# Attention units of one PSUM bank in a fused attention and gated MLP kernel

## The chip, the cores and the metric

The kernel runs on one core of a Trainium2 chip. The metric is the time of the device in microseconds (us). Five engines work beside each other and meet only at semaphores: TensorE (PE: matmuls; PEld: its weight loads), VectorE (DVE), ScalarE (ACT), GpSimd (POOL), and SyncE (SP), which issues the DMAs. A PSUM bank is here a tile of 128 partitions by 512 float32 values; eight of them are allotted.

## The reference

Attention over 4 batches of 8 heads, 1152 keys and values of 64 numbers each; queries are averaged in pairs, which leaves 576. Its output feeds a gated MLP with a residual (cut to what matters):

```python
q_pool = q.reshape(B, H, S // 2, 2, D).mean(axis=3)           # 4, 8, 576, 64
scores = scale * q_pool @ k.transpose(0, 1, 3, 2)             # 576 x 1152 per head
attn = softmax(scores)                                         # over the 1152 keys
x = (attn @ v) -> (B, 576, 512)
u, v = split(gelu(x @ w_in))                                   # 512 each
v_s = einsum("ts,bsd->btd", w_sg, layernorm(v) * g_ln) + b_sg
out = x + (u * v_s) @ w_out
```

## The kernel before

**Units.** The 32 heads stand in 16 pairs p of two heads. A head's 1152 keys are KJ = 9 tiles of 128. One step of attention, `attend(g)`, is a head with one key tile j, so g runs over 288 units. A unit holds all 576 queries, in a score tile of two PSUM banks with 288 columns in each (pool "S", two tiles of two banks). TensorE writes the scores in two passes, `scores(0)` and `scores(1)` (line 450), the second of which adds low-order parts and subtracts each query's maximum; ScalarE takes the exponential (line 458). In pairs 0 and 2 (`F32P`, "wide") the exponential stays float32 and TensorE weighs v with it (line 496, five blocks of 128 queries). In the other pairs it is split into two float16 parts: ScalarE makes the first (line 472, into a tile f of pool "F"), and the second, the residual, is made on VectorE for every other unit, which is "kept": its exponential is written back into the score tile, which stays taken until the residual is done. For the rest the exponential goes to a tile e of pool "E" in SBUF, the score tile is free after it, and GpSimd makes the residual (both line 477). TensorE then weighs v with both parts (line 489, 15 matmuls per unit) into one bank, `avp`, which sums a head's nine units and is emptied by ScalarE (line 523), divided on VectorE and GpSimd.

The 576 queries are four blocks of 128 and a last of 64. In the unit before, the 64 lead the row, so that the fifth block is a 128-column slice that starts with them.

**What goes before a unit.** For each pair: loads of k, q, v (`load`), scales (`scales`), splitting k, q and v in two parts (`prepare`, lines 319 to 340 on ScalarE, VectorE and SP; `values`, 362 and 365), transposition by DMA, a copy of k's second half, and the maxima (`maxima`): TensorE writes 128 x 512 raw scores into a bank (line 389), VectorE reduces it (line 395, tile mp), GpSimd splits the maximum, and a DMA transposes it into q2, without which `scores(1)` can't start.

**Other work.** The gated MLP of a batch (`project`, `gmlp`, matmuls in `unit`, line 634) is mixed into the attention of the next one; only that of the last batch stands alone at the end. At the start `spatial` loads and splits the gate weights w_sg (line 880 and on; residuals on VectorE in line 947) and `weights` splits w_in and w_out.

**Order.** Nothing runs in the order of the source. `Schedule.add` notes each piece with an engine, an estimated duration, what it reads and writes, a due time and a pool from which it takes a buffer; `Schedule.run` then plays all engines forward and always starts the ready piece with the earliest due time. The engine queues are fixed by that before the kernel runs. The due times come from the tables D_... at the end of the file (`lead`), one number per kind of work and pair. The pieces "sseq", "eseq", "fseq" and "avp" keep scores, exponentials, first parts and weighing each in the order of the units. The banks of PSUM: `avp` 1, S 2 x 2, X 2 (maxima, transpositions, MLP), M 1.

## Time and profile before

| | |
|---|---|
| median of 3 runs | 675.05 us (673.8 to 675.7) |
| span of the profiled execution | 671.1 us |
| median less that span | 3.95 us |
| busy: TensorE, VectorE, ScalarE, GpSimd | 630.2, 531.6, 520.0, 365.4 us |
| mean granted clock of TensorE | 0.997 |

For the profiled execution the page gives the span, from its first to its last instruction, and no time of its own beside it; the difference to the median stands in the third line. Busy times are sums over the span: an engine that is 79% busy over the whole can be full for 50 us. A TensorE that counts as busy is not at its peak, since ends of matmuls are modelled; the spacing of starts tells more. Idle time of an engine matters only where the engine that ends the stretch waits for it.

### The profile page before, as it was taken

The numbers are of one execution on the slowest core, as the hardware profiler recorded it, in microseconds if no ns is written. First come the engines' busy times: TensorE is split into PE (matmuls) and PEld (weight loads), VectorE is DVE, ScalarE is ACT, GpSimd is POOL, SyncE is SP. The second block draws the span as 40 slices with busy tenths as digits, with TensorE's granted clock in tenths as the row PEclk, the third lists the DMA queues.
The fourth block names the chain that finished last, engine by engine and source line by source line (L and its number), as shares of the span: only waits on it lengthen the run. The fifth ranks groups of instructions, "written<-read, shape, count | busy, mean of one in ns | idle before, by whom it ended". The sixth has DMA issues, their size and how long they took to land.

```text
span 671.1 us, 18518 instructions
## 1 busy us (share of the span) xinstructions
PE 630.2 (94%) x7498; PEld 492.5 (73%) x7498; DVE 531.6 (79%) x1066; ACT 520.0 (77%) x851; POOL 365.4 (54%) x425
## 2 busy tenths in 40 slices
PE   3889879988999999999999999999999999999997
PEld 1578658966777876867777986687777976887955
DVE  4979999798988997888988898888888897243462
ACT  6477988699989789889999888978987797773220
POOL 6243865547464558736465556874444467640172
PEclk9899999999999999999999999999999999999999
DMA  8797847544443315655356223529333200010002
GB/s 231 206 246 161 218 70 213 123 80 111 127 97 84 77 22 143 105 143 126 88 130 144 48 72 66 110 71 220 79 68 72 49 11 17 7 49 23 1 1 71
DMA packets 110133, 66.78 MB, mean 100 GB/s; under 512 B 88480, under 2 KB 92576, under 8 KB 109920
## 3 DMA queue, kind: packets, MB, share of 16 engines
q1 hardware_dynamic: 110048, 65.61, 41.3%
q8 instruction: 58, 0.95, 0.6%
q14 instruction: 27, 0.22, 0.1%
HBM read 36.23 MB, written 4.72 MB: 61 GB/s over the span
## 4 chain that ended last, share of the span: by engine, by line
PE 68%; DVE 15%; ACT 7%; DMA 5%; issue 3%; POOL 2%; SPq 0%; ACTq 0%; POOLq 0%; DVEq 0%
PE s L450 15%; PE pm L634 13%; PE avp L489 12%; PE px L634 11%; PE px L389 7%; DVE mp L395 5%; PE avp L496 4%; DVE f L477 2%; DMA k<-kn 2%; ACT f L472 2%; ACT e L458 1%; ACT s L458 1%; DMA kr<-in_k_dram 1%; DVE va L365 1%; DVE t L673 1%
## 5 line engine op out<-in xcount | busy, mean ns | idle before, releaser
L477 POOL TENSOR_TENSOR f<-e,f 128x576 f16<-128x576 f32 x126 | 166.2, 1319 | 139.2 <-ACT f L472 128.7
L450 PE MATMUL s<-q,k 128*128 128x288 f16 (+2 forms) x1440 | 216.4, 262 | 10.4 <-ACT e L458 6.3
L395 DVE TENSOR_REDUCE mp<-px 128x1 f32<-128x512 f32 (+2 forms) x304 | 193.0, 661 | 23.1 <-PE px L389 22.8
L489 PEld LDWEIGHTS <-f 128*128 128x128 f16 x3780 | 147.4, 97 | 24.1 <-issue 3.8
L489 PE MATMUL avp<-va,f 128*128 128x65 f16 x3780 | 157.1, 193 | 2.3 <-POOL f L477 1.8
L450 PEld LDWEIGHTS <-k 128*128 128x128 f16 x1440 | 105.0, 98 | 67.2 <-issue 34.6
L477 DVE TENSOR_TENSOR f<-s,f 128x576 f16<-128x576 f32 x126 | 94.4, 749 | 37.3 <-ACT f L472 37.2
L389 PE MATMUL px<-k,q 128*128 128x512 f16 (+1 forms) x437 | 114.8, 326 | 7.5 <-DVE mp L395 5.2
L458 ACT ACTIVATE e<-s 128x576 f32<-128x576 f32 x162 | 104.8, 648 | 18.7 <-PE s L450 13.2
L458 ACT ACTIVATE s<-s 128x576 f32<-128x576 f32 x126 | 81.1, 644 | 36.5 <-PE s L450 35.3
L472 ACT ACTIVATE f<-e 128x576 f16<-128x576 f32 x126 | 86.7, 688 | 4.1
L472 ACT ACTIVATE f<-s 128x576 f16<-128x576 f32 x126 | 81.9, 650 | 2.6 <-PE avp L489 0.5
L389 PEld LDWEIGHTS <-q 128*128 128x128 f16 x480 | 43.0, 100 | 21.8 <-issue 12.0
L496 PEld LDWEIGHTS avp<-va,e 128*128 128x128 f32 x360 | 43.7, 192 | 2.1 <-ACT a L523 1.2
L496 PE MATMUL avp<-va,e 128*128 128x65 f32 x360 | 44.4, 271 | 0.4 <-ACT a L523 0.4
L314 POOL TENSOR_TENSOR qs<-qr 128x256 f32<-128x256 f32 x32 | 25.6, 801 | 34.9 <-DVE n L336 19.5
L634 PE MATMUL pm<-win_h,xg 128*128 128x512 f32 x104 | 38.7, 417 | 0.0
L634 PEld LDWEIGHTS <-vz 128*128 128x128 f16 x224 | 20.5, 98 | 19.3 <-POOL vz L681 1.1
L530 POOL TENSOR_TENSOR x<-a,dn 128x320 f32<-128x320 f32 x32 | 25.7, 803 | 15.9 <-DVE dn L527 14.0
L634 PE MATMUL px<-wsg,vz 128*128 128x512 f16 x126 | 32.5, 379 | 0.8 <-POOL vz L681 0.6
L634 PE MATMUL pm<-xg,win_h 128*128 128x288 f32 x144 | 31.1, 308 | 0.7 <-DVE u L606 0.7
L322 DVE SCALAR_TENSOR_TENSOR kn<-kr,sc,kn 128x576 f16<-128x576 f32 x32 | 28.8, 909 | 1.4 <-ACT kn L319 1.4
(162 smaller groups left out, 1095.3 us busy)
## 6 DMA issues: line engine op xcount, KB each, us to landing
kr<-in_k_dram SPq DMA_DIRECT2D x16, 576.0 KB, 4.7
qr<-in_q_dram SPq DMA_DIRECT2D x16, 512.0 KB, 4.1
vr<-in_v_dram SPq DMA_DIRECT2D x14, 576.0 KB, 4.0
k<-k SPq DMA_DIRECT2D x32, 144.0 KB, 2.6
x<-in_moe_w_in_dram SPq DMA_DIRECT2D x8, 512.0 KB, 5.9
out_dram<-t SPq DMA_DIRECT2D x16, 256.0 KB, 2.1
x<-in_moe_w_out_dram SPq DMA_DIRECT2D x8, 256.0 KB, 3.2
u<-in_moe_w_sg_dram SPq DMA_DIRECT2D x1, 1152.0 KB, 6.5
```

Of the source, the lines that this page charges most:

```text
L314: nc.gpsimd.tensor_tensor(out=qs[:, 6 * h:6 * h + 4, :], in0=qr[:, h, :, 0, :], in1=qr[:, h, :, 1, :], op=ALU.add)
L322: nc.vector.scalar_tensor_tensor(out=kn[:, h, :, 1, :], in0=kr[:, h], scalar=s[:, 0:1], in1=kn[:, h, :, 0, :], op0=ALU.mult, op1=ALU.subtract)
L389: nc.tensor.matmul(out=bank(x)[:, w * i:w * i + w], lhsT=q1[c][:, o, :], rhs=k1[c][:, h, j0:j0 + nj, :].rearrange("p j k -> p (j k)"), sta ...
L395: nc.vector.tensor_reduce(out=mp[c][:, r0:r0 + len(group), g], in_=src, axis=AX.X, op=ALU.max)
L450: nc.tensor.matmul(out=buf(("s", g))[:, a, to:to + n], lhsT=kk[c][:, hh, j, :], rhs=qq[:, at:at + n], start=(i == 0 and to == 0), stop=(i ...
L458: nc.scalar.activation(out=s if kept else halves(buf(("e", g))), in_=s, func=AF.Exp, scale=SCALE * 2.0**-ASH)
L472: nc.scalar.activation(out=f, in_=exponentials(), func=AF.Copy)
L477: eng.tensor_tensor(out=halves(f[:, 1]), in0=exponentials(), in1=halves(f[:, 0]), op=ALU.subtract)
L489: nc.tensor.matmul(out=avp[:, o:o + m], lhsT=w[:, col:col + 128], rhs=vv, start=(j == 0 and n == 0 and x == 0), stop=(j == KJ - 1 and n == ...
L496: nc.tensor.matmul(out=avp[:, o:o + D + 1], lhsT=e[:, col:col + 128], rhs=vj, start=(j == 0 and n == 0), stop=(j == KJ - 1 and n == 4), sk ...
L530: nc.gpsimd.tensor_tensor(out=xbuf[b % 2][:, :, col], in0=a[:, :, 0:D], in1=d.rearrange("p (i o) -> p i o", o=1).to_broadcast([128, 5, D]) ...
L634: nc.tensor.matmul(out=bank(m)[:, 0:cols], lhsT=l, rhs=r, start=(k + j == 0), stop=(k + j == n - 1))
```

## The change

A unit is now one bank: 512 queries of a key tile. The last 64 queries are gathered over key tiles: after j = 4 a tail unit takes those of tiles 0 to 4 side by side (320 columns), after j = 8 those of tiles 5 to 8 (256 columns). A head thus has 11 units, 9 main and 2 tail. Each tail block brings its own k tile as weights in the score matmuls and its own v tile in the weighing. Every other main unit is kept as before; tail units never are (`KEEPT`), so their residuals are made on GpSimd. A slice of 128 columns at the end of a tail unit reaches 64 columns beyond it, into columns that must hold numbers: GpSimd sets columns 256 to 383 of all E and F tiles to zero once at the start (`clear`), and the first score pass of every unit waits for it.

The seven banks beside `avp` become seven tiles of one bank, 3 S, 3 X and 1 M, in place of two pairs and three. All due times of the tables are new, so the queues of all engines stand in another order.

```diff
-        "S": tiles(psum, 2, [128, 2, 512], F32, "s"),
+        "S": tiles(psum, NPS, [128, 512], F32, "s"),
         "X": tiles(psum, NXB, [128, 512], F32, "px"),
-        "M": tiles(psum, 3 - NXB, [128, 512], F32, "pm"),
+        "M": tiles(psum, 7 - NPS - NXB, [128, 512], F32, "pm"),
...
     def attend(g):
         h, j = divmod(g, KJ)
         p, hh = divmod(h, 2)
...
+        main(g, h, p, hh, j)
+        if j in TAILS:
+            j0 = max([0] + [a + 1 for a in TAILS if a < j])
+            unit_of(("t", g), g + TOFF, h, p, hh, [(i, 4, 64 * (i - j0)) for i in range(j0, j + 1)])
+        if j < KJ - 1:
+            return
+        heads_end(g, h, p, hh)
+
+    def main(g, h, p, hh, j):
+        unit_of(g, g, h, p, hh, [(j, i, 128 * i) for i in range(4)])
+
+    def unit_of(u, g, h, p, hh, blocks):
...
+        tail = blocks[0][1] == 4
+        n = 64 * len(blocks) if tail else TM
+        o = (704 if hh else TM) if tail else 768 * hh
...
-            parts = [(0, 0, o, HALF), (1, 0, o + HALF, HALF)] if hh else [(0, 0, TM, TT), (0, TT, 0, HALF - TT), (1, 0, HALF - TT, HALF)]
-            for a, to, at, n in parts:
-                nc.tensor.matmul(out=buf(("s", g))[:, a, to:to + n], lhsT=kk[c][:, hh, j, :], rhs=qq[:, at:at + n],
-                                 start=(i == 0 and to == 0), stop=(i == 1 and to + n == HALF), skip_group_check=True)
+            for m, (j, _, col) in enumerate(blocks if tail else blocks[:1]):
+                w = TT if tail else TM
+                nc.tensor.matmul(out=buf(("s", u))[:, col:col + w], lhsT=kk[c][:, hh, j, :], rhs=qq[:, o:o + w],
+                                 start=(i == 0 and m == 0), stop=(i == 1 and col + w == n), skip_group_check=True)
...
-        kept = not wide and share(g, KEEP[p >= NP])
+        kept = not wide and (share(int(g), KEEP[p >= NP]) if not tail else KEEPT)
...
+        def clear():
+            for t in pools["F"]:
+                nc.gpsimd.memset(t[:, :, 256:384], 0.0)
+            for t in pools["E"]:
+                nc.gpsimd.memset(t[:, 256:384], 0.0)
...
-D_LK = (-94.74, -97.1, -50.09, -46.73, -13.16)
+D_LK = (-874.76, -83.67, 106.62, 781.44, 481.99)
...
-NXB = 2
+NXB = 3
+NPS = 3
+TAILS, TOFF, KEEPT = (4, 8), 0.5, False
```

Exponential, first part, residual and weighing run over the n columns of a unit and, in the weighing, over its blocks; else they are as before.

Three places show what the new table does to the queues. The first is VectorE's queue where pair 3 ends and pair 4 begins: f is the unit's float16 tile, s its score tile, kn and n2 the second parts of the next pair's k and q, mp the reductions, pm and sc the scales. Before:

```order
L477 TENSOR_TENSOR f3_131<-s0_134,f3_131 128x576
L322 SCALAR_TENSOR_TENSOR kn_94<-kr_90,sc2_106,kn_94 128x9x64
L336 SCALAR_TENSOR_TENSOR n2_85<-qs_83,sc2_106,n1_84 128x5x64 x2
L395 TENSOR_REDUCE mp1_82<-px1_137 128x1
L271 TENSOR_SCALAR pm1_103<-pm0_138 128x1
L272 TENSOR_SCALAR pm1_103<-pm1_103 128x1
L293 RECIPROCAL sc5_109<-pm1_103 128x1
L296 TENSOR_SCALAR sc5_109<-sc5_109 128x1
L395 TENSOR_REDUCE mp1_82<-px0_136 128x1
L395 TENSOR_REDUCE mp1_82<-px1_137 128x1
L477 TENSOR_TENSOR f1_129<-s1_135,f1_129 128x576
```

And now, from the same residual (the 18th that VectorE makes):

```order
L482 TENSOR_TENSOR f2_130<-s2_136,f2_130 128x512
L859 SCALAR_TENSOR_TENSOR x1_89<-x1_89 128x256
L862 SCALAR_TENSOR_TENSOR x1_89<-x1_89 128x256
L482 TENSOR_TENSOR f1_129<-s0_134,f1_129 128x512
L533 TENSOR_SCALAR dn1_115<-a1_113,sc3_107 128x5
L534 RECIPROCAL dn1_115<-dn1_115 128x5
L364 SCALAR_TENSOR_TENSOR va0_86<-vr_91,sc4_108,va0_86 128x9x64
L482 TENSOR_TENSOR f3_131<-s2_136,f3_131 128x512
L335 SCALAR_TENSOR_TENSOR n2_85<-qs_83,sc2_106,n1_84 128x5x64 x2
L321 SCALAR_TENSOR_TENSOR kn_94<-kr_90,sc2_106,kn_94 128x9x64
```

The two residuals, the 18th and the 19th, stood nine rows apart; now two short ones on w_out's parts (x1) stand between them, and the parts of q and k come after the 20th.

The second is SP's queue at the start of the program, where kr, qr, qe and va are k, q, q's last rows and v of pair 0, and the rows from in_moe_w_sg to g_ln are the gate's. Before:

```order
L240 DMA kr_90<-in_k_dram 128x2x576
L243 DMA qr_92<-in_q_dram 128x2x512
L246 DMA qe_93<-in_q_dram 64x128 x2
L880 DMA u_97<-in_moe_w_sg_dram 128x2304
L883 DMA x1_89<-in_moe_w_sg_dram 64x576
L884 DMA x1_89<-in_moe_b_sg_dram 128x576
L885 DMA graw_141<-in_moe_g_ln_dram 128x4x1
L340 DMA_TRANSPOSE q10_77<-n1_84 128x5x128
L326 DMA_TRANSPOSE k10_73<-kn_94 128x9x128 x2
```

And now:

```order
L239 DMA kr_90<-in_k_dram 128x2x576
L895 DMA u_97<-in_moe_w_sg_dram 128x2304
L898 DMA x1_89<-in_moe_w_sg_dram 64x576
L899 DMA x1_89<-in_moe_b_sg_dram 128x576
L900 DMA graw_143<-in_moe_g_ln_dram 128x4x1
L242 DMA qr_92<-in_q_dram 128x2x512
L245 DMA qe_93<-in_q_dram 64x128 x2
L253 DMA va0_86<-in_v_dram 128x9x64 x2
L325 DMA_TRANSPOSE k10_73<-kn_94 128x9x128
```

The loads of q moved behind those of the gate, and the load of v came ahead of the first transposition.

The third is ScalarE's queue in pair 4: e<-s and s<-s are exponentials, f<-s and f<-e first parts; the number behind s is the score tile. Before:

```order
L458 ACTIVATE s1_135<-s1_135 128x2x288
L472 ACTIVATE f3_131<-s1_135 128x576
L458 ACTIVATE e2_126<-s0_134 128x576
L841 ACTIVATE x1_89<-x1_89,ebias_64 128x256
L472 ACTIVATE f0_128<-e2_126 128x576
L458 ACTIVATE s0_134<-s0_134 128x2x288
L472 ACTIVATE f1_129<-s0_134 128x576
L458 ACTIVATE e1_125<-s1_135 128x576
L472 ACTIVATE f2_130<-e1_125 128x576
```

And now:

```order
L471 ACTIVATE e0_124<-s1_135 128x512
L477 ACTIVATE f0_128<-e3_127 128x320
L471 ACTIVATE s0_134<-s0_134 128x512
L856 ACTIVATE x1_89<-x1_89,ebias_64 128x256
L477 ACTIVATE f1_129<-e0_124 128x512
L471 ACTIVATE e1_125<-s1_135 128x512
L477 ACTIVATE f2_130<-s0_134 128x512
L471 ACTIVATE s2_136<-s2_136 128x512
```

Two score tiles took turns; now three do, and a first part of a tail (320 columns) stands among those of 512.

## Rows read from the trace of the kernel before

**Rows 1.** Page, engines: busy us (share of the span) xinstructions.

```profile
PE 630.2 (94%) x7498; PEld 492.5 (73%) x7498; DVE 531.6 (79%) x1066; ACT 520.0 (77%) x851; POOL 365.4 (54%) x425
```

**Rows 2.** Stretches: span; busy us (x) of PE, PEld, DVE, ACT, POOL; granted clock, DMA, GB/s.

```profile
0.00:13.90 13.90, 3.02 (x17) 2.56 (x18) 4.87 (x22) 9.54 (x14) 8.75 (x14) 1.00 0.83 245
13.90:50.00 36.10, 31.95 (x211) 21.91 (x210) 32.23 (x66) 19.92 (x34) 13.45 (x20) 0.95 0.89 220
50.00:97.30 47.30, 41.49 (x530) 33.45 (x531) 45.23 (x88) 40.02 (x67) 28.49 (x36) 1.00 0.66 154
97.30:167.00 69.70, 63.10 (x755) 52.03 (x752) 59.93 (x126) 57.86 (x101) 41.49 (x52) 1.00 0.54 129
167.00:607.30 440.30, 433.02 (x5651) 339.39 (x5650) 361.80 (x715) 378.18 (x619) 254.14 (x289) 1.00 0.37 86
607.30:671.00 63.70, 57.57 (x342) 43.22 (x340) 27.52 (x53) 14.44 (x19) 19.09 (x17) 1.00 0.07 23
```

**Rows 3.** Waits: engine, line waited for: us in total, times, longest us.

```profile
PE s L450 <- ACT e L458: 6.3, 11, 1.2
...
PE px L389 <- DVE mp L395: 5.2, 8, 1.8
...
PE s L450 <- DVE f L477: 3.4, 9, 0.8
```

**Rows 4.** Timeline of TensorE at 401 us: start, us, instruction, tiles, shape, count.

```profile
401.21 0.62 PE L489 MATMUL avp<-va,f 128*128 128x65 f16 x15
401.67 0.41 PE L450 MATMUL s<-q,k 128*128 128x288 f16 x2
401.92 0.38 PE L389 MATMUL px<-k,q 128*128 128x512 f16 x1
402.13 0.44 PE L489 MATMUL avp<-va,f 128*128 128x65 f16 x9
```

**Rows 5.** VectorE's groups by shape: line, tiles, shape, count; busy us, mean ns; idle before.

```profile
L395 DVE TENSOR_REDUCE mp<-px 128x1 f32<-128x512 f32 x259 | 170.6, 681 | 21.1 <-PE px L389 20.9
L477 DVE TENSOR_TENSOR f<-s,f 128x576 f16<-128x576 f32 x126 | 94.4, 749 | 37.3 <-ACT f L472 37.2
L322 DVE SCALAR_TENSOR_TENSOR kn<-kr,sc,kn 128x576 f16<-128x576 f32 x32 | 28.8, 909 | 1.4 <-ACT kn L319 1.4
...
L336 DVE SCALAR_TENSOR_TENSOR n<-qs,sc,n 128x320 f16<-128x320 f32 x32 | 23.6, 748 | 2.6 <-DMA q<-n 1.4 <-ACT n L332 1.1
```

**Rows 6.** Timeline of VectorE, residuals 9, 18 and 19, and TensorE's wait between.

```profile
96.53 0.74 DVE L477 TENSOR_TENSOR f<-s,f 128x576 f16<-128x576 f32 x1
...
160.45 0.76 DVE L477 TENSOR_TENSOR f<-s,f 128x576 f16<-128x576 f32 x1 [1.63 <-ACT f L472]
...
166.24 0.75 DVE L477 TENSOR_TENSOR f<-s,f 128x576 f16<-128x576 f32 x1
...
164.54 0.38 PE L389 MATMUL px<-k,q 128*128 128x512 f16 x1 [1.19 <-DVE mp L395]
```

**Rows 7.** ScalarE's and GpSimd's groups by shape, columns as in rows 5.

```profile
L458 ACT ACTIVATE e<-s 128x576 f32<-128x576 f32 x162 | 104.8, 648 | 18.7 <-PE s L450 13.2 <-PE avp L496 3.6 <-DVE f L477 0.8
...
L523 ACT ACTIVATE a<-avp 128x325 f32<-128x325 f32 x32 | 14.1, 442 | 3.1 <-PE avp L489 3.1
...
L477 POOL TENSOR_TENSOR f<-e,f 128x576 f16<-128x576 f32 x126 | 166.2, 1319 | 139.2 <-ACT f L472 128.7 <-PE s L450 8.3 <-POOL qs L316 1.3
...
L850 POOL TENSOR_TENSOR x<-x 128x256 f32<-128x256 f32 x8 | 6.1, 764 | 6.7 <-DVE x L847 6.7
```

**Rows 8.** Timeline of the start: TensorE, GpSimd, and one row of VectorE.

```profile
13.90 0.58 PE L389 MATMUL s<-k,q 128*128 128x512 f16 x1 [0.86 <-DMA k<-kn]
...
6.28 0.72 POOL L314 TENSOR_TENSOR qs<-qr 128x256 f32<-128x256 f32 x1 [4.41 <-DMA qr<-in_q_dram]
...
8.73 2.01 POOL L782 MEMSET k<- 64x2304 f16 x1
...
21.11 0.74 DVE L947 SCALAR_TENSOR_TENSOR wsg<-px,wsc,wsg 128x512 f16<-128x512 f32 x1
```

More of the change, by code (lines that the diff above doesn't have):

```diff
@@ L463, in exponentials @@
         def exponentials():
[L465 removed]
+            return (buf(("s", u)) if kept else buf(("e", u)))[:, 0:n]
         def exp_hi():
[L468 to L472 removed]
+            nc.scalar.activation(out=buf(("f", u))[:, 0, 0:n], in_=exponentials(), func=AF.Copy)
@@ L492, in weigh_wide @@
         def weigh_wide():
-            e, vj = buf(("e", g)), vw[c][:, KJ * hh + j, :]
-            for n, (i, col) in enumerate(blocks):
+            e = buf(("e", u))
+            for k, (j, i, col) in enumerate(blocks):
                 o = (D + 1) * i
-                nc.tensor.matmul(out=avp[:, o:o + D + 1], lhsT=e[:, col:col + 128], rhs=vj, start=(j == 0 and n == 0),
-                                 stop=(j == KJ - 1 and n == 4), skip_group_check=True)
-        hi_dve = not kept and share(g, E1F[p >= NP])
@@ L500, in attend @@
-        home = ("s", g) if kept else ("e", g)
-        add("PE", 0.246, lambda: scores(0), r=[f"k1{c}{hh}", f"q1{c}{hh}"] + ([f"q1{c}0"] if hh else []), w=["sseq", f"s{g}"], due=g - 0.8,
-            acq=(("s", g), ["S"]))
-        add("PE", 0.246, lambda: scores(1), r=[f"k2{c}{hh}", f"q2{c}{hh}", f"k2z{c}"], w=[f"s{g}"], due=g - 0.7)
+                nc.tensor.matmul(out=avp[:, o:o + D + 1], lhsT=e[:, col:col + 128], rhs=vw[c][:, KJ * hh + j, :],
+                                 start=(j == 0 and k == 0 and not tail), stop=(j == KJ - 1 and tail), skip_group_check=True)
```

106 lines of the change are left out of this document (53 added, 53 removed).

## The prediction

> **What bounds the kernel now.** I read the busy times first, then the span cut into stretches, then the waits, and last two close-ups. TensorE is busy 630.2 of 671.1 us [rows 1], so at most 40.9 us can be won without taking matmuls away, and the change takes hardly any. The question is only where TensorE stands idle and what it waits for there. The stretches [rows 2] give its idle time as length minus busy: 10.9 us before the first maxima at 13.9; 4.2 from there to 50; 5.8 from 50 to 97.3; 6.6 from 97.3 to 167; 7.3 in the 440 us from 167 to 607.3; 6.1 in the closing gated MLP. From 50 to 167 VectorE is busy 45.2 + 59.9 = 105.2 of 117.0 us, nearly full; after 167 it has 78 us free and TensorE is the bound almost alone. I chose 97.3 and 167 because there the 9th and the 19th residual that VectorE makes (line 477) end [rows 6]; the weighing matmuls of those units can't run before them.
>
> The waits [rows 3] say what TensorE waits for: a score tile that ScalarE has not yet read (6.3 us), a score tile that VectorE holds until its residual is done (3.4 us), and a bank whose maximum is not yet reduced (5.2 us). All three are shortages of PSUM banks or lateness of VectorE. 14.9 us together is the size of what this change is about.
>
> **The change, part by part.**
>
> *Scores on TensorE.* A key tile had 2 x 576 columns in four to six matmuls; now it has 2 x 512 in two and 2 x 64 in two. By start spacing [rows 4] two matmuls of 288 take 401.92 - 401.67 = 0.25 us, one of 512 takes 402.13 - 401.92 = 0.21, and one of 65 columns with its own weights, the nearest to the new 64, takes 0.46 / 15 = 0.031. Before 2 x 0.25 = 0.50 per key tile, after 2 x 0.21 + 2 x 0.031 = 0.482. The columns are the same 1152, and 0.01 us is what the rows resolve, so I take 0; the other end is 288 x 0.018 = 5.2 us saved. The weighing matmuls keep their number (3780 and 360).
>
> *VectorE up to 167 us.* I counted its order up to the 19th kept residual. Before: 98 reductions, 12 second parts of k, 12 of q, 9 of v, 19 residuals. Now 95, 10, 10, 8 and 19 with 512 columns for 576. A residual goes from 749 ns to about the 681 of the 512-column reduction [rows 5]: 19 x 0.068 = 1.3 us. The rest: 3 x 0.681 = 2.0, 2 x 0.909 = 1.8, 2 x 0.748 = 1.5, and one part of v at the price of one of k, 0.9. Together 7.5 us less in front of that residual (four steps on w_out and some of one column, also fewer, I leave unpriced); this work isn't gone, it is done later, where VectorE has 78 us free [rows 2], and without that cover it would come back one for one. The close-up [rows 6] shows the mechanism: between the 18th residual (160.45) and the 19th (166.24) VectorE had a part of k, two of q, three reductions and four short steps, and TensorE stood 1.19 us for a reduction at 164.54; now two short steps stand between them. TensorE's own matmuls up to that unit are the same. The gain lies between 0 and the 5.8 + 6.6 = 12.4 us that TensorE is idle there. I take the 7.5, since VectorE is the full engine of this stretch. After it ScalarE and TensorE's own order are late next.
>
> *A third score tile and a third X bank.* Three one-bank score tiles replace two pairs, so a tile is asked for again after three units instead of two, and reductions have one bank more. After 167 us the gain lies between 0 and the 7.3 us of idle time; I take 3, under half, since part of that idle time follows other waits.
>
> *The head.* SP now issues the gate weights, their bias and v ahead of or around q, and POOL sets both halves of k2 and the eight pads to zero before it pools q. The gate weights and bias are 1.18 + 0.15 + 0.29 = 1.62 MB; at 245 GB/s [rows 2] q lands 6.6 us later than the 6.28 us at which POOL has it now [rows 8], near 12.9. POOL's four memsets at 2.0 us [rows 8] are over near 10, so they hide in that wait; without it they would cost up to 8. The first maximum starts at 13.90 now, and its last wait is for k, not for q [rows 8]; so a part of q's 6.6 us is absorbed. Between 0 and 6.6 I take the middle, 3.3: the first maximum near 17. In return four of the six gate-weight residuals (line 947, 0.74 us each [rows 8]) and their turns on TensorE now fill that wait; before they stood in VectorE's full stretch, at 21.11 and later: 4 x 0.74 = 3.0 us given back. Net +0.3. [...]
>
> *More and shorter instructions.* ScalarE gets 64 more exponentials and 56 more conversions with no column more. From 576 columns at 648 ns and 325 at 442 [rows 7] a column costs 0.82 ns and an instruction 175 ns, so at most 120 x 0.175 = 21 us, at least 0 where one starts under the end of another. ScalarE has 11.8 us free from 97.3 to 167 and 62 us after [rows 2]; these hide it, and without them 21 us would be on the path. POOL's residuals: 126 shrink by 64 columns, 56 of 256 to 320 columns are new. From 1319 and 764 ns [rows 7] a column costs 1.73 ns: -126 x 0.11 + 28 x (0.764 + 0.875) = +32 us on an engine with 28 us free from 97.3 to 167 and 186 after. Both cost 0 in the sum, and up to the rival below.
>
> [...]
>
> *The closing gated MLP* has the same matmuls in the same order: 0.
>
> **The sum.** 0 (scores) - 7.5 (VectorE) - 3 (banks) + 0.3 (head) = -10.2 on a span of 671.1: 660.9. The median of the runs, 675.05, is 3.95 above that span; I keep that distance: 664.9 us.
>
> **Rivals.**
> *The moved work was hidden (same).* TensorE's idle time from 50 to 167 may come from the chain score, exponential, conversion, residual and not from VectorE's load. For it: from 97.3 to 167 VectorE is free 9.8 us itself. Against: TensorE's longest wait there is for a reduction. Then -3 + 0.3 at best and +0.3 at worst: 672.4 to 675.4.
>
> *The head is late (slower).* q lands 6.6 us later, and VectorE is nearly full from 14 to 97 us, so a late start is not made up before TensorE takes over. It decides if the first maximum starts more than the given-back 3.0 us after 13.9, so after 17. Then up to +6.6, with a third of the gain after 167 left: 671.1 + 6.6 - 1 = 676.7, so 680.7. Against it: the wait is filled.
>
> *ScalarE becomes the bound (slower).* It is 86% busy after 167 (378 of 440). If the 440 of 671 us share of the 21 us, 13.8, ended on the path, and only the 7.5 before were won: 677.4, so 681. It decides where ScalarE has no idle slice left in a stretch dense in attention. [...]
>
> *Both gains in full.* -12.4 and -7.3 with the same head: 651.7, so 655.7. For it: lateness of VectorE and shortage of banks are the named waits.
>
> **Chances.** Forecast 0.55 (658 to 671); both gains in full 0.12; hidden 0.14; late head 0.12; ScalarE 0.07. The range: about half of the full-gain case lies below 655, and of the two slower ones some 0.10 above 680; 655 to 680 is left, which takes in the ends of each term but not all of them at once. About 0.3%, 2 us, is what a measurement of this kernel can tell from no change. Faster by more (under 673): 0.55 + 0.12 + a fifth of the hidden case = 0.70; within, the rest of that case: 0.11; slower: 0.19.
>
> **What would show it.** In the profile after: 19th kept residual ends near 159 instead of 167; TensorE's idle time from 50 us to there under 6 us; the three waits of rows 3 together under 9 us; first maximum near 17, and the 9th kept residual no later than 97. Wrong, if the first maximum is at 19 or later, if ScalarE is above 95% busy in a 40 us stretch, or if TensorE now waits for POOL's residuals by more than 5 us.

## The result: 678.4 us, slightly slower

The changed kernel takes 678.36 us (median of 11 runs, 673.58 to 680.74) against 674.46 for the kernel before (11 runs beside them): ratio 1.0053, 95% interval 1.0032 to 1.0074. I had forecast 664.9 and given 0.70 to faster. A ratio leaves out executions more than 1.5% above the fastest of their kernel and a median doesn't, so the two can differ (most in qpin, tailshort, actshort and noload). The profiled run is a long one, 680.74 us with a span of 678.9; its span is 7.8 us over that of before.

Engines and the six stretches of rows 1 and 2, now of the kernel after (busy us and instructions of PE, PEld, DVE, ACT, POOL; granted clock; DMA share; GB/s):

```profile
PE 635.7 (94%) x7210; PEld 458.0 (67%) x7210; DVE 530.3 (78%) x1066; ACT 521.0 (77%) x971; POOL 396.0 (58%) x489
```

```profile
0.00:13.90 13.90, 4.73 (x25) 4.05 (x25) 3.75 (x20) 9.04 (x14) 12.85 (x23) 1.00 0.91 254
13.90:50.00 36.10, 29.25 (x126) 20.44 (x127) 27.64 (x55) 17.20 (x28) 10.77 (x17) 0.68 0.84 199
50.00:97.30 47.30, 44.85 (x503) 33.59 (x502) 41.01 (x80) 37.36 (x73) 26.66 (x32) 0.96 0.74 146
97.30:167.00 69.70, 64.55 (x768) 49.04 (x767) 61.74 (x131) 60.09 (x119) 42.91 (x57) 1.00 0.46 113
167.00:607.30 440.30, 426.76 (x5365) 301.15 (x5362) 366.57 (x727) 381.35 (x719) 281.84 (x343) 1.00 0.42 89
607.30:678.90 71.60, 65.58 (x437) 49.72 (x433) 29.59 (x56) 15.95 (x22) 20.97 (x19) 1.00 0.08 26
```

Two rows stand out against rows 2: from 13.9 to 50 the granted clock is 0.68 (it was 0.95), and from 167 to 607.3 TensorE's idle time is 440.30 - 426.76 = 13.5 us (it was 7.3). To see where time goes I follow when ScalarE empties the weighing bank at the end of a head. Heads 0, 7 and 31, before (line 523), then after (line 530):

```profile
49.57 0.43 ACT L523 ACTIVATE a<-avp 128x325 f32<-128x325 f32 x1
...
163.62 0.42 ACT L523 ACTIVATE a<-avp 128x325 f32<-128x325 f32 x1
...
607.05 0.44 ACT L523 ACTIVATE a<-avp 128x325 f32<-128x325 f32 x1 [2.40 <-PE avp L489]
```

```profile
60.27 0.44 ACT L530 ACTIVATE a<-avp 128x325 f32<-128x325 f32 x1
...
166.26 0.43 ACT L530 ACTIVATE a<-avp 128x325 f32<-128x325 f32 x1
...
614.85 0.44 ACT L530 ACTIVATE a<-avp 128x325 f32<-128x325 f32 x1 [6.06 <-PE avp L491]
```

Head 0 ends 10.7 us later. Head 7 (the middle rows) ends at 166.7, before at 164.0, so 8.0 us were won between them. From head 7 to head 31 it takes 448.60 us against 443.45, 5.2 us lost; the closing part is unchanged. Each profile is one execution: for the same way, in the order of the changed kernel, fill (below) takes 449.80 and a long execution of qpin (684.25 us) 454.84. Start, middle and the way behind head 7 are three separate questions.

**The start.** TensorE's first maximum, GpSimd and the memsets ahead of its pooling (rows 8):

```profile
17.77 0.63 PE L388 MATMUL s<-k,q 128*128 128x512 f16 x1
```

```profile
7.78 2.02 POOL L789 MEMSET k<- 64x2304 f16 x1
9.85 2.01 POOL L790 MEMSET k<- 3x2304 f16 x1
11.95 0.72 POOL L313 TENSOR_TENSOR qs<-qr 128x256 f32<-128x256 f32 x1
```

The first maximum starts at 17.77, where I had 17. q had landed at 11.40 (I had 12.9) and GpSimd's memsets were over at 11.86 (I had 10), so pooling began at 11.95. TensorE had gate transpositions in front of the maximum and waited 1.19 us at 16.85 for VectorE's gate residuals. But the second score pass starts only 1.5 us later than before (31.46 against 29.98); what makes head 0 long lies behind it. Stretches of the kernel after, columns as above, cut where the granted clock changes:

```profile
16.58:19.99 3.41, 3.14 (x10) 1.71 (x11) 3.08 (x6) 1.85 (x4) 0.38 (x1) 0.50 1.01 243
19.99:30.23 10.24, 6.24 (x26) 2.12 (x25) 10.14 (x23) 2.38 (x4) 2.30 (x7) 1.00 1.05 237
30.23:50.71 20.48, 19.83 (x90) 16.32 (x90) 11.92 (x25) 10.91 (x19) 7.42 (x9) 0.50 0.74 183
```

TensorE is busy 6.24 of 10.24 us up to 30.23, waiting for VectorE's reductions; then the clock is at 0.50 for 20.48 us with TensorE busy 19.83 of it. With 3.41 us before and 3.41 at 81.4 it is 27.3 us at half clock; the kernel before had 3.41 us (26.18 to 29.59).

**The three waits** of rows 3 now, and others that are new or longer:

```profile
PE px L288 <- ACT kn L285: 8.1, 3, 6.0
PE s L463 <- DVE f L482: 4.8, 14, 0.8
PE px L388 <- DVE mp L394: 3.5, 8, 0.7
PE avp L491 <- DVE f L482: 3.4, 3, 2.1
PE s L463 <- DMA q<-n: 3.0, 4, 1.3
...
PE s L463 <- ACT e L471: 1.4, 4, 0.6
...
PE avp L491 <- POOL f L482: 1.1, 5, 0.3
```

The three fell from 14.9 to 4.8 + 3.5 + 1.4 = 9.7 us, as banks that come free sooner would make it. In their place TensorE waits for the q2 transposition (3.0), for ScalarE's squares of k (8.1, of which 6.0 stand at the start, 5.9 before) and, in the weighing, for VectorE's residuals (3.4; 2.1 of it at 81 us, 1.1 at 143).

**Residuals 9 and 19** on VectorE (rows 6) and the step that runs between 18 and 19:

```profile
101.12 0.68 DVE L482 TENSOR_TENSOR f<-s,f 128x512 f16<-128x512 f32 x1
...
161.22 1.76 DVE L364 SCALAR_TENSOR_TENSOR va<-vr,sc,va 128x576 f16<-128x576 f32 x1
...
165.37 0.69 DVE L482 TENSOR_TENSOR f<-s,f 128x512 f16<-128x512 f32 x1 [0.92 <-ACT f L477]
```

From the 9th to the 19th it takes 166.06 - 101.80 = 64.3 us, before 166.99 - 97.27 = 69.7. The middle row, a second part of v, comes up again below.

**POOL's residuals** by shape (busy us, mean ns; rows 7 had 166.2 us in 126):

```profile
L482 POOL TENSOR_TENSOR f<-e,f 128x512 f16<-128x512 f32 x126 | 150.9, 1199 | 99.9 <-ACT f L477 84.9 <-PE px L388 3.5 <-issue 3.4
...
L482 POOL TENSOR_TENSOR f<-e,f 128x320 f16<-128x320 f32 x28 | 24.0, 858 | 8.1 <-ACT f L477 6.2 <-DMA qr<-in_q_dram 1.8
L482 POOL TENSOR_TENSOR f<-e,f 128x256 f16<-128x256 f32 x28 | 20.7, 739 | 10.5 <-ACT f L477 8.9 <-PE px L388 0.8 <-PE avp L491 0.5
```

195.6 us, 29 more, as sized (+32).

### The profile page after: what moved, and what is told of

Read it like the earlier page. It is cut to its first block, busy times and chain, and to the rows that moved or that the text cites. A ratio compares the mean times of both kernels' runs of the same rounds, so it can differ in the third digit from the quotient of the medians.

```text
span 678.9 us, 18196 instructions
## 1 busy us (share of the span) xinstructions
PE 635.7 (94%) x7210; PEld 458.0 (67%) x7210; DVE 530.3 (78%) x1066; ACT 521.0 (77%) x971; POOL 396.0 (58%) x489
## 4 chain that ended last, share of the span: by engine, by line
PE 42%; DVE 28%; ACT 12%; DMA 10%; issue 6%; POOL 2%; SPq 1%; ACTq 0%; DVEq 0%; POOLq 0%
PE px L641 11%; PE s L463 10%; DVE mp L394 9%; PE avp L491 8%; PE pm L641 4%; PE px L388 4%; DVE f L482 4%; DMA q<-n 3%; ACT f L477 3%; PE avp L498 3%; DMA kr<-in_k_dram 2%; DVE va L364 2%; ACT e L471 2%; DVE kn L321 2%; ACT s L471 2%
## 5 line engine op out<-in xcount | busy, mean ns | idle before, releaser
L482 POOL TENSOR_TENSOR f<-e,f 128x512 f16<-128x512 f32 (+2 forms) x182 | 194.8, 1076 | 118.4 <-ACT f L477 100.0
L463 PE MATMUL s<-q,k 128*128 128x512 f16 (+1 forms) x1152 | 231.5, 290 | 10.7 <-DVE f L482 4.8
L471 ACT ACTIVATE e<-s 128x512 f32<-128x512 f32 (+2 forms) x226 | 123.8, 549 | 43.3 <-PE s L463 32.4
L477 ACT ACTIVATE f<-e 128x512 f16<-128x512 f32 (+2 forms) x182 | 105.6, 583 | 4.4 <-PE avp L491 3.4
L482 DVE TENSOR_TENSOR f<-s,f 128x512 f16<-128x512 f32 x126 | 86.0, 683 | 24.6 <-ACT f L477 18.0
L477 ACT ACTIVATE f<-s 128x512 f16<-128x512 f32 x126 | 76.5, 607 | 7.8 <-PE avp L491 4.5
L471 ACT ACTIVATE s<-s 128x512 f32<-128x512 f32 x126 | 76.2, 604 | 4.8 <-PE s L463 4.0
L388 PEld LDWEIGHTS <-q 128*128 128x128 f16 x480 | 42.3, 100 | 31.1 <-issue 10.7
L641 PE MATMUL px<-win_h,xg 128*128 128x512 f32 x136 | 50.4, 423 | 0.1
L313 POOL TENSOR_TENSOR qs<-qr 128x256 f32<-128x256 f32 x32 | 26.3, 823 | 27.3 <-DVE n L335 22.2
L641 PE MATMUL px<-wout_h,xg 128*128 128x512 f32 x104 | 39.5, 422 | 0.0
L641 PE MATMUL px<-xg,win_h 128*128 128x288 f32 x152 | 32.7, 307 | 0.0
```

Of the source, the lines that this page charges most:

```text
L313: nc.gpsimd.tensor_tensor(out=qs[:, 6 * h:6 * h + 4, :], in0=qr[:, h, :, 0, :], in1=qr[:, h, :, 1, :], op=ALU.add)
L388: nc.tensor.matmul(out=bank(x)[:, w * i:w * i + w], lhsT=q1[c][:, o, :], rhs=k1[c][:, h, j0:j0 + nj, :].rearrange("p j k -> p (j k)"), sta ...
L463: nc.tensor.matmul(out=buf(("s", u))[:, col:col + w], lhsT=kk[c][:, hh, j, :], rhs=qq[:, o:o + w], start=(i == 0 and m == 0), stop=(i == 1 ...
L471: nc.scalar.activation(out=s if kept else buf(("e", u))[:, 0:n], in_=s, func=AF.Exp, scale=SCALE * 2.0**-ASH)
L477: nc.scalar.activation(out=buf(("f", u))[:, 0, 0:n], in_=exponentials(), func=AF.Copy)
L482: eng.tensor_tensor(out=f[:, 1, 0:n], in0=exponentials(), in1=f[:, 0, 0:n], op=ALU.subtract)
```

## Experiments

Every run stands against runs of the kernel before taken beside it; ratios are to those. The kernel's planner makes its whole order anew when one number changes, so most edits keep the changed kernel's order and alter one thing in it. One kernel that took all due times behind the first pair from before, *oldsteady*, shows why: 708.7 us, with the order of all engines different. It says nothing on the units.

### Is it the start?

*fill* adds, in the maxima of the first pair:

```
+ if p == 0:
+     nc.tensor.matmul(out=avp, lhsT=unit_b, rhs=ones_b, start=True, stop=True)
```

> Edit: behind every maxima matmul of the first pair TensorE gets one more matmul of 512 columns into the weighing bank, whose result the first weighing overwrites; nothing else moves. It only keeps TensorE busy between about 18 and 31 us, where it waits for VectorE's reductions. Theory A (the granted clock): the 20.5 us at level 0.5 from 30 to 51 follow from TensorE's waiting just before; with the filler the level is 1.0 from 20 us on, head 0 ends near 51 instead of 60.5, and the time falls by 3 to 8 us, to 670 to 675. Theory B (the late q is what costs): the clock is a side matter, head 0 ends later than 58, the time stays within 2 us of 678.4. Theory C (the loss lies behind 167 us): whatever head 0 does, the time moves by under 2 us.

Measured: 677.45 us, ratio 1.0044 (1.0017 to 1.0070). The stretches of its profile:

```profile
19.99:30.23 10.24, 9.62 (x43) 3.94 (x42) 9.75 (x20) 1.26 (x2) 2.61 (x7) 1.00 0.89 238
30.23:50.71 20.48, 19.72 (x155) 14.67 (x154) 19.83 (x44) 16.67 (x30) 9.86 (x10) 1.00 0.79 190
50.71:81.43 30.72, 28.13 (x241) 23.11 (x240) 20.82 (x43) 19.58 (x39) 14.71 (x18) 0.83 0.84 172
```

With TensorE busy 9.62 of the 10.24 us, the half-clock stretch is gone from where it was and head 0 ends at 53.5. One profile would prove little, since the clock differs from execution to execution. But in twelve profiles (the changed kernel and eleven others below), in which TensorE's queue at the start is that of the changed kernel, a stretch at half clock begins between 28.0 and 30.9 us each time; in fill none begins before 63. That TensorE's waiting brings this fall is so far well supported. How long the stretch lasts is another matter: 3.4 to 27.3 us in the twelve, with the same queue. In taildve, normact and pooltiny, which have 6.8 us at half clock up to 51 where the profile of the changed kernel has 23.9, head 0 ends at 51.9, 52.1 and 52.5, against 60.7 there and 50.0 before the change. So some 2 us of the 10.7 remain without the long stretch.

In fill 10 us at half clock come later (0.83 from 50.7 to 81.4). Of the 7.3 us by which head 0 ends sooner 3.1 are left at head 7 and 1.9 at head 31. A's mechanism stands, its size does not.

*qpin* moves six steps of the first pair ahead (q's loads, pooling, scaling and first transposition); *oldhead* takes the first entry of each table from before:

> Edit: the changed kernel in its own order, but in the first pair the q loads are issued before the gate loads, q is pooled before the second half of k2 is set to zero, q is scaled before the gate weights are squared, and the first q transposition is issued before the first of k. Theory B (late q costs): the first maximum starts 2 to 4 us sooner (14 to 16 instead of 17.8), and that comes through to the end: 674.5 to 676.5. Theory A (clock): the start of the maxima hardly matters; unless the stretch at level 0.5 behind 30 us shrinks, head 0 still takes about 29 us from the second score pass to its end and the time stays at 676.5 to 680. Theory C: under 2 us of change.

> Edit: the new units, with the due times, start times and gate order of the kernel before for the first pair alone (first entry of each table, and the R and SG numbers). The greedy order is made anew from there, so later queues shift too. Theories A and B: first maximum near 14, the gate transposes back between the maxima, at most 3.4 us at level 0.5, head 0 ends at 50 to 53, the time 668 to 674. Theory C (what is lost is lost behind 167 us): head 7 still ends at 163 to 167, the time 675 to 680. If the 8.0 us won from head 0 to head 7 come from VectorE having worked ahead while TensorE ran at half speed, head 7 also ends at 163 to 167, and the time is 673 to 676.

Measured: qpin 678.0 us, ratio 1.0018 (0.9996 to 1.0041), oldhead 680.67, ratio 1.0073 (1.0055 to 1.0091). qpin did not do what it was for. In its profile the gate transpositions still stand in front of the first maximum in TensorE's queue, and now wait for their data:

```profile
12.60 0.82 PE L972 MATMUL px<-ident,x 64*128 64x64 f32 x5 [5.80 <-DMA x<-in_moe_w_sg_dram]
...
20.99 0.63 PE L413 MATMUL s<-k,q 128*128 128x512 f16 x1
```

The first maximum starts 3.2 us later than in the changed kernel, not sooner, and head 0 still ends 5.3 us sooner (55.35), with 6.8 us at half clock before 50. So the start of the first maximum is not what makes head 0 long; what an early q is worth, qpin doesn't tell.

In oldhead head 7 ends at 160.2, 6.5 us sooner than in the changed kernel, and from there to head 31 it takes 456.15 us: all of it is given back and 1 us more. But its order behind the start is made anew as well, so the loss can be that of the new order. fill, which keeps the order, points the same way: most of what was won at the start is lost again by head 31.

**The clock over all runs.** Each run lists its span and mean granted clock, so its time at half clock is 2 x (1 - clock) x span (the profiles of the two kernels show the levels 1.00 and 0.50 and no other). Of the 11 runs of the changed kernel, seven at 0.979 to 0.984 (22 to 28 us at half clock) have a median of 678.6 us, four at 0.987 to 0.991 one of 676.2. Over 109 runs of the 14 kernels with the new start, each kernel with a level of its own, a microsecond at half clock goes with 0.31 us of time (95% interval 0.26 to 0.36); I take 0.30. The changed kernel has a median of 25.7 us, variants of the kernel before 6 to 7. So (25.7 - 6.5) x 0.30 = 5.8 us of its time go with the clock. Taken run by run, which goes by its mean of 21.9 us, it would at 6.5 us stand about 1 us below the kernel before. I give such estimates, against the kernel before, as "at equal clock": -1.1 us for the changed kernel, -6.6 for tailshort, -14.0 for poolshort, -4.5 for actshort, each good to some 1.5 us. That the clock is the cause of this spread is inferred from it, not shown by an edit: fill had a median of 13.5 us at half clock, for which 0.30 x 12.2 = 3.7 us would be expected, and gained 0.9 us.

### Is it GpSimd?

*poolshort* and *tailshort* cut its residuals, all or those of the tails:

```
+ m = n if kept or p < 3 else 64          # poolshort
+ m = 64 if tail and p >= 3 else n        # tailshort
- eng.tensor_tensor(out=f[:, 1, 0:n], in0=exponentials(), ...)
+ eng.tensor_tensor(out=f[:, 1, 0:m], in0=exponentials()[:, 0:m], ...)
```

> Edit: the changed kernel in its own order, but from the fourth pair on POOL makes its residuals for 64 columns only (the rest of the second part keeps old data): about 1.0 us less for each of the 512-column ones, some 120 us less POOL work. Rival U on POOL (its 32 us more, and the preparation steps that queue behind its residuals, make TensorE wait): the time falls by 4 us or more. Theory P with transfers as its cause: under 2 us, since the waits for POOL's residuals are 2.9 us in all and run beside others.

> Edit: the changed kernel in its own order; from the fourth pair on POOL makes the residual of the 64-query tails for 64 columns only, in place of 320 and 256 (the rest keeps old data). That takes back about 26 of the 32 us by which the change loads POOL more. Theory S (POOL's added instructions make VectorE's instructions with two SBUF inputs wait: behind 167 us they are stretched by 35 us over their undisturbed length, 26 before the change): the stretch falls to 27 to 30 us, the way from head 7 to head 31 from 448.6 to 442 to 445, the time by 3.5 to 7 us, to about the kernel before. Rival D (preparation is late because of the transfers, POOL's load of before was just as costly): under 2 us.

Measured: poolshort 664.75 us, ratio 0.9836 (0.9802 to 0.9871); tailshort 674.02, ratio 0.9963 (0.9935 to 0.9992). Head 7 to head 31 as one stretch, columns as above, first of before, then after, tailshort, poolshort:

```profile
163.80:607.25 443.45, 434.96 (x5675) 340.52 (x5674) 364.89 (x724) 381.27 (x624) 256.81 (x294) 1.00 0.38 87
```

```profile
166.46:615.06 448.60, 434.88 (x5460) 307.46 (x5456) 368.88 (x731) 383.35 (x723) 283.68 (x345) 1.00 0.41 89
```

```profile
161.48:607.44 445.96, 433.23 (x5460) 307.10 (x5456) 361.88 (x731) 383.39 (x723) 264.26 (x345) 1.00 0.41 89
```

```profile
165.37:605.03 439.66, 431.27 (x5460) 306.77 (x5456) 351.99 (x731) 381.90 (x723) 171.52 (x345) 1.00 0.40 91
```

Compare before with after: TensorE's busy time is the same, POOL has 27 us more, and 5.2 us are lost. Taking 19 us of POOL's work away gives back 2.6 of them in this stretch, a difference of two single executions; over all runs the ratio falls by 0.009 (6 us; 5 by the medians, 5.5 at equal clock), which is clear of noise. The same rows show VectorE: 731 instructions in all three, but 368.88, 361.88 and 351.99 us busy. Its groups show which instructions stretch, after and then poolshort (of before, the step on v alone, last):

```profile
L394 DVE TENSOR_REDUCE mp<-px 128x1 f32<-128x512 f32 x269 | 174.8, 680 | 25.2 <-PE px L388 23.5 <-PE px L288 0.6
...
L364 DVE SCALAR_TENSOR_TENSOR va<-vr,sc,va 128x576 f16<-128x576 f32 x28 | 29.4, 1060 | 0.1
```

```profile
L394 DVE TENSOR_REDUCE mp<-px 128x1 f32<-128x512 f32 x269 | 175.5, 682 | 25.7 <-PE px L388 23.8 <-PE px L288 0.6
...
L364 DVE SCALAR_TENSOR_TENSOR va<-vr,sc,va 128x576 f16<-128x576 f32 x28 | 23.0, 832 | 0.1
```

```profile
L365 DVE SCALAR_TENSOR_TENSOR va<-vr,sc,va 128x576 f16<-128x576 f32 x28 | 27.3, 990 | 0.5 <-ACT va L362 0.5
```

A reduction from PSUM takes 680 to 682 ns beside either load; the second part of v, with two inputs in SBUF, takes 832 ns on a relieved POOL and 1060 on a loaded one (990 before the change), 1.76 us in the row at 161.22 above. POOL's row there:

```profile
161.21 1.16 POOL L482 TENSOR_TENSOR f<-e,f 128x512 f16<-128x512 f32 x1 [0.85 <-ACT f L477]
```

The residual starts 0.01 us before the step on v and ends 1.15 us into it; the step ends 0.61 us later. The 28 steps on v in this profile fall into two groups: 15 take 0.78 to 0.82 us, and the other 13, at 0.88 to 1.81 us, each end 0.61 or 0.62 us after a GpSimd instruction that began before the step or at most 0.03 us behind it. So such a step waits for GpSimd's instruction within its own time, and the engines do not meet only at semaphores, as I had written ahead of the prediction, which priced nothing of the kind.

Two mirror runs on the kernel before: *poolshort_b* cuts its residuals alike, *morepool_b* makes POOL repeat a part of each (`f[:, 1, 0:128]`, p >= 3).

> Edit: the kernel before the change, in its own order, but from the fourth pair on POOL makes its residuals for 64 of the 576 columns only (the rest keeps old data), about 115 us less POOL work. If POOL's load was no cost before and became one with the change: under 3 us, 672 or more. If it was a cost before too, and the change adds to it (34 us more POOL work in the old kernel cost 8 us): 5 to 11 us less, 664 to 670, about where the changed kernel with short residuals ended (664.8), and then the units themselves are worth nothing either way.

> Edit: the kernel before the change, in its own order, but from the fourth pair on POOL makes the first 128 columns of each of its residuals a second time: 104 more instructions of about 0.33 us, 34 us more on POOL, as much as the change adds. Theory S: the same cost comes to the old kernel: VectorE's stretch behind 167 us rises from 26 to 33 to 38 us, the time by 3 to 8 us, to 678 to 683. Rival D, or the cost belongs to the new units alone: under 1.5 us.

Measured: poolshort_b 669.57 us, ratio 0.9911 (0.9882 to 0.9939); morepool_b 683.82, ratio 1.0119 (1.0091 to 1.0146). Head 7 to head 31 of morepool_b, and whom TensorE waits for there:

```profile
165.75:616.12 450.37, 436.42 (x5675) 341.22 (x5674) 363.20 (x723) 382.28 (x624) 307.84 (x402) 1.00 0.38 85
```

```profile
PE avp L491 <- POOL f L479: 8.5, 18, 1.0
```

POOL's load cost the old kernel 6 us already, and 51 us more of it cost 8; each residual with its repeated part is done 1.87 us after its start there, 1.32 in the kernel before, and TensorE waits for it. The changed kernel pays 14.7 (0.9836 against 1.0053; 12.9 at equal clock). With the residuals cut in both, the changed kernel takes 0.9836 / 0.9911 = 0.992 of the old, 5 us less (2 to 8), 8 at equal clock. That is the worth of units, banks and due times together; no run separates them. As far as the profiles show, it is not won behind head 7. The row of poolshort_b:

```profile
166.18:604.18 438.00, 432.90 (x5675) 340.18 (x5673) 346.47 (x721) 380.53 (x624) 149.85 (x292) 1.00 0.38 87
```

Cutting the residuals wins 448.60 - 439.66 = 8.9 us of this way in the changed kernel and 443.45 - 438.00 = 5.4 in the old one, so 3.5 of the 5.2 us lost there are POOL's; with both cut, the new kernel is still 1.7 us behind.

### How does GpSimd's load cost?

The expectations speak of VectorE's stretch. That is the sum, over its instructions from 163 to 616 us, of what each takes beyond the short ones of its kind (their 8th percentile): 26.0 us before the change, 35.0 after, 26.7 in tailshort, 15.1 in poolshort. In morepool_b it is 23.9: it did not rise, as theory S wanted; the old kernel paid for the load in direct waits for POOL's residuals. In poolshort_b the stretch falls by 20 us, to 5.9, and the time by 6.

*pooltiny* and *pooltiny2* are poolshort with one-column instructions behind each short residual, so that POOL is occupied but never for long; the second, shown here, has fewer:

```
+ if m < n:
+     for _ in range(1 if tail else 5):
+         eng.tensor_tensor(out=f[:, 1, 0:1], in0=exponentials()[:, 0:1], in1=f[:, 0, 0:1], op=ALU.subtract)
```

> Edit: as the run with POOL's residuals cut to 64 columns from the fourth pair on (which was about 13 us faster than the changed kernel), but behind each of them POOL runs one-column instructions, 6 for 512 columns, 4 for 320, 3 for 256, so that POOL is occupied about as long as by the full residual. Theory S as a lock held for one instruction: VectorE waits only for a short one, its stretch stays under 20 us, the time 664 to 669. Rival Q (what matters is that steps queue behind POOL's residuals, such as the maxima's split and the pooling of q): 674 to 680, as in the changed kernel.

> Edit: as the earlier run with POOL's residuals cut to 64 columns and one-column instructions behind them from the fourth pair on, but with 5 behind a 512-column unit and 1 behind a tail in place of 6 and 3 to 4. There POOL was busy 327.6 us between head 7 and head 31 (292.2 in the changed kernel) with VectorE's stretch at 17.6 us (35.0); at about 0.19 us each it should now be 280 to 295, so POOL's occupancy is that of the changed kernel and only the long instructions are gone. [...] Theory Q (steps in POOL's own queue come late: residuals, the maxima's split, the pooling of q): 675 to 682.

Measured: pooltiny 710.96 us, ratio 1.0546 (1.0505 to 1.0588). It had more load than meant: POOL's instructions add up to 327.6 us from 163 to 616 us, where the changed kernel has 292.2 (the next expectation calls that stretch head 7 to head 31). VectorE's stretch was 17.6 us. pooltiny2 took 683.93 us, ratio 1.0119 (1.0090 to 1.0147); VectorE's stretch 17.9. From head 7 to head 31, and TensorE's longest wait:

```profile
166.80:618.98 452.18, 434.68 (x5460) 308.29 (x5456) 355.20 (x731) 383.28 (x723) 288.97 (x929) 1.00 0.40 88
```

```profile
PE avp L495 <- POOL f L486: 11.7, 24, 1.3
```

VectorE is relieved (355.20 us, near poolshort's 351.99) at about POOL's old occupancy, and nothing is won. But the edit puts in a wait of its own: a 512-column unit's residual with its one-column instructions is done 1.78 us after its start, where the full residual took 1.20, and TensorE now waits 11.7 us for residuals, 1.1 in the changed kernel. If these 10.6 us are all on the path, pooltiny2 would stand near 673 without them, below the changed kernel; so theory S is not refuted, and not shown either. What is shown is that POOL's work on residuals costs. By which way, VectorE's stretch or steps that come late in POOL's own queue, and how much by each, stays open.

### ScalarE, transfers, VectorE

*actshort* (exponentials and conversions of 384 in place of 512 columns), *noload* (no k, q and v loads from the fifth pair on), *noload_b* (the same on the kernel before):

```
+ m = n if p < 3 or tail else 384         # actshort, both activations
+ if p >= 4:                              # noload, in lk, lq, lv and lv_wide
+     return
```

> Edit: the changed kernel in its own order, but from the fourth pair on the exponentials and conversions of the 512-query units cover 384 columns (the rest keeps old data): about 0.1 us less for each of some 420 instructions, 44 us less work on ScalarE with the same number of instructions. Rival U on ScalarE (it is 87% busy behind 167 us, and its 120 more instructions are paid on the path): the time falls by 4 us or more. Theory P: under 2.5 us, what earlier squares bring.

> Edit: the changed kernel in its own order, but from the fifth pair on k, q and v are not loaded (the steps work on the data of earlier pairs). That takes the loads away from the transpositions they collide with: behind 167 us a k transposition takes 5.2 us to land in the changed kernel and 3.4 in the one before. Theory P with transfers as its cause: the transpositions land in under 3.2 us, the waits for them and for k's squares go, the time falls by 4 to 8 us. If preparation is late for another reason (VectorE, POOL, order): under 2 us. Rival U: under 2 us.

> Edit: the kernel before the change, in its own order, without the loads of k, q and v from the fifth pair on; the same edit made the changed kernel about 10 us faster, to 0.990 of the kernel before. If the transfers cost the changed kernel more (its k transpositions land after 5.2 us, those of before after 3.4): under 4 us less, 671 or more. If loads cost both kernels alike, and so explain nothing of the difference: 7 to 12 us less, 663 to 668.

Measured: actshort 678.21 us, ratio 1.0014 (0.9986 to 1.0042), about the changed kernel's time (3 us better at equal clock). From head 7 to head 31 ScalarE is busy 36 us less and the way is no shorter, 449.18 us: the loss there is not ScalarE's. noload 670.05, ratio 0.9896 (0.9867 to 0.9925); noload_b 672.75, ratio 0.9954 (0.9938 to 0.9971). Issues of the k transposition from 167 to 607 us (count, median us to landing), before, after and noload:

```profile
k<-kn SPq DMA_TRANSPOSE x20, 3.4
```

```profile
k<-kn SPq DMA_TRANSPOSE x22, 5.2
```

```profile
k<-kn SPq DMA_TRANSPOSE x22, 3.3
```

The new order issues transpositions into loads, and loads cost it 10.6 us against 3.1. From head 7 to head 31 noload wins 448.60 - 442.95 = 5.7 us and noload_b 443.45 - 440.98 = 2.5, so 3.2 of the 5.2 us lost there go with the loads. With POOL's 3.5 that is more than was lost: the two overlap, probably because both edits take away the same waits for late preparation, or they are within what single executions differ by.

Four ways to move work, each keeping the whole result: the tails' residuals to VectorE (*taildve*), the split of the maxima to VectorE (*splitdve*), the division of the heads to ScalarE (*normact*), two steps of the split to ScalarE (*splitact*).

```
+ eng = nc.vector if kept or tail else nc.gpsimd                                        # taildve
- nc.gpsimd.tensor_scalar(out=nm, ...)    + nc.vector.tensor_scalar(out=nm, ...)        # splitdve, and two more
+ nc.scalar.activation(out=xbuf[...][:, i, col], in_=a[:, i, 0:D], scale=d[:, i:i + 1]) # normact, i in 0..4
+ nc.scalar.activation(out=nm, in_=nm, func=AF.Copy, scale=1.0 / MW)                    # splitact, and the copy
```

> Edit: the changed kernel in its own order, but the residuals of the 64-query tails are made by VectorE in place of POOL, all of them, complete. VectorE gets 56 instructions of about 0.4 us, 22 us more, and POOL loses 39 us. Theory S: POOL is off VectorE's back for 39 us, and VectorE has 75 us free behind 167; the time falls by 2 to 6 us, to 672 to 676. [...]

> Edit: the changed kernel in its own order, but the three short steps that scale and split the negated maxima (line 424 to 426, 0.67 us per half pair on POOL, with up to 2 us of queue ahead of them) run on VectorE. POOL loses 21 us, VectorE gets about 10, and the q2 transposition starts sooner. Theories S and Q both: the time falls by 2 to 6 us, to 672 to 676, and the waits for the q2 transposition (3.1 us) go. Rival V (VectorE's queue is as long): 677 to 681.

> Edit: the changed kernel in its own order, but the product of a head's sums with the reciprocals of its denominators (POOL, one instruction of 0.77 us per head) runs on ScalarE as five instructions of 64 columns, about 0.24 us each. POOL loses 25 us, ScalarE gets about 38, and 44 us less on ScalarE had made no difference. If POOL's load is what costs and ScalarE has room: 672 to 676. If ScalarE, held up by the denominators in front of its exponentials, costs as much: 678 to 690.

> Edit: the changed kernel in its own order, but two of the three short steps on the negated maxima (lines 424 and 425) run on ScalarE, the third stays on POOL. POOL loses 14 us, ScalarE gets 32 + 32 short instructions, about 13 us, VectorE none. POOL's load costing: 674 to 677. If every engine's queue is as tight as VectorE's (10 us more there had cost 11): 680 to 688.

Measured: 680.49 us (ratio 1.0071, 1.0046 to 1.0095), 689.53 (1.0209), 696.22 (1.0303) and 685.60 (1.0144). None wins: the last three are slower than the changed kernel (1.0053), and taildve can't be told from it. In splitdve TensorE's wait for reductions grows from 3.5 to 12.3 us (the row of its waits, then the stretch from head 7 to head 31):

```profile
PE px L388 <- DVE mp L394: 12.3, 16, 2.0
```

```profile
160.67:622.46 461.79, 439.29 (x5466) 309.41 (x5465) 385.31 (x798) 383.54 (x723) 266.84 (x279) 0.99 0.38 86
```

From head 7 to head 31 VectorE is busy 385.31 us against 368.88 and idle for 76; yet 16 us more on it, in steps that the q2 transposition waits for, cost 11. No version with the whole result beat the kernel before.

*nowait* was a miss. TensorE was to read q1 in place of q2 and a constant for the squares, so as not to wait for them:

> Edit: the changed kernel in its own order, but from the fourth pair on the second score pass reads the first q half (q1) in place of the transposed second half (q2), and the one-column sum of the squares reads a constant; so TensorE waits neither for the q2 transposition nor for ScalarE's squares there. Both steps still run; the scores and scales are wrong. Theory P (the loss behind 167 us is preparation that comes just in time: 3.1 us for q2 and 3.7 for the squares, 0.6 in the kernel before): the time falls by 5 to 9 us, to 669 to 673, and the way from head 7 to head 31 from 448.6 to 440 to 443. Rival U (more and shorter instructions on ScalarE and POOL make every step later): the waits move to the next step of the chain, the time falls by under 3 us, to 675.5 or more.

Measured: 683.53 us, ratio 1.0118 (1.0082 to 1.0154). TensorE's wait for transpositions of q rose from 3.0 to 7.8 us. As I read it, q1 is read longer and so the next transposition into it waits, a wait that I had put in myself; the run decides nothing.

## Why the prediction was wrong

- *First maximum near 17*: 17.77, near, but with luck: q came sooner than I had it and the memsets later, and the last thing in front of the maximum were gate transpositions, which I had counted as filling. It is just past the point at which my rival "the head is late" was to decide. Its time (680.7) is near the result, but by another mechanism: the lateness of q reached the second score pass with 1.5 us only, and in qpin head 0 ended sooner although the first maximum started later.
- *The head, +0.3*: head 0 ends 10.7 us later in the profiled run, some 2 of them where the half-clock stretch is short.
- *The granted clock*: the sum has no term for it, the first failed step. There were 27 us at half clock in the profiled run, and by the slope over the runs 5.8 us of the median go with it (inferred; fill, the one edit on it, won 0.9). In the kernel before, gate transpositions fill TensorE's wait for reductions at 27.7 to 31 us. The order showed that they move ahead of the first maximum; I counted that as a gain for VectorE and did not price what TensorE's waiting leaves behind. That TensorE's waiting brings the fall is supported for the one near 30 us (twelve profiles against fill), not for the later ones, and why it lasts 3.4 us in one execution and 27.3 in another stays open.
- *VectorE up to the 19th residual, -7.5*: right in kind. From head 0 to head 7 it is -8.0 us, from the 9th to the 19th residual -5.5; but it starts 4.5 us late, so the 9th ends at 101.80 and not by 97, the 19th at 166.06 and not near 159. The parts of v in front of the 19th were 6 and 5, not 9 and 8; the difference of one, which the sum uses, holds. That the -8.0 comes of VectorE's lighter queue is not tested by an edit. TensorE's idle time from 50 to there is 7.4 us (116.06 - 108.70), forecast under 6, before 12.4.
- *Banks, -3*: the three waits fell by 5.2 to 9.7 us, forecast under 9. That this won 3 us is not shown: behind head 7 the new kernel loses 5.2 us, and with POOL's residuals cut in both kernels it is still not the faster one there (439.66 against 438.00).
- *POOL's +32 us "cost 0"*: the second failed step, and the one that edits show. 29 us came, and the tails' residuals are worth 6 us (tailshort); cutting all of POOL's residuals wins 14.7 us now and 6.0 before. I covered it with 186 us of idle time. The sign that I had set, TensorE waiting over 5 us for POOL's residuals, didn't show (1.1 us). The rows show a longer VectorE instead (368.88 us, 361.88 without the tails' residuals); whether that is the way by which the cost reaches TensorE is not shown.
- *"VectorE has 78 us free" behind 167 us*: false as a cover. 16 us more there cost 11.
- *ScalarE, 120 instructions at 0*: right. Its busy time rose by 1.0 us, and cutting its columns left the median where it was. It passed my 95% mark in one stretch (38.03 of 40 us from 200 to 240) without harm that the runs could show.
- *Scores on TensorE, 0*: right within what the rows tell; head 7 to 31 has the same busy time, 434.9.

As an account at equal clock: units, banks and order -14.0 + 6.0 = -8, POOL's load (14.0 - 1.1) - 6.0 = +6.9, clock +5.8, together +4.7 against 678.36 - 674.46 = 3.9 measured. That the sum comes near is no test of the shares: the first two add up to the changed kernel's own -1.1 whatever poolshort and poolshort_b took, and that -1.1 is the measured difference less the clock's share. The shares are estimates; that of the loads overlaps with them, and how far stays open.

## To carry to other kernels

Idle time was no cover on an engine whose queue is in a fixed order with every step just in time (16 us more on VectorE, idle for 76, cost 11): before booking added work at nothing, look at who waits for what stands behind it in that queue, and which instructions of another engine its own wait for (here 13 of the 28 steps on v). When work that fills an engine's waiting time is moved away, price the clock of the stretch that follows (27.3 us at half clock here, 3.41 before). And a kernel tuned to one machine-made order is best studied by edits that keep this order (the two that made it anew, oldhead and oldsteady, were slower than the kernel before). Then look in the profile whether such an edit moved what it was to move (qpin didn't) and whether it put in a wait of its own (pooltiny2 and nowait did).

## What was new on the hardware

- The same program ran with 12 to 28 us at half clock from run to run, and in the profiled one the granted clock stayed at 0.50 for 20.48 us in which TensorE was busy for 19.83. In twelve profiles with the same queue the fall near 30 us came each time and lasted 3.4 to 27.3 us.
- VectorE's two-input step on 576 SBUF columns took 832 ns on average on a relieved POOL and 1060 on a loaded one, while PSUM reductions stayed at 680 to 682; short POOL instructions in place of long ones relieved VectorE (355.20 us busy against 368.88). In the profile of the changed kernel 13 of the 28 steps on v ended 0.61 or 0.62 us after a POOL instruction; the other 15 took 0.78 to 0.82 us.
- A one-column POOL instruction took 210 ns on average (637 in pooltiny2), against 1199 for 512 columns.
